# A hand-written issue order redone: fp32 products ahead of the first up-projection, and up-projections listed apart from their relu

## The chip, the cores and the metric

The program runs on one core of a Trainium2 chip. The metric is device time in microseconds (us), lower is better. A core has five engines that each work through their own list of instructions in order: TensorE (PE in the profile, its weight loads PEld), VectorE (DVE), ScalarE (ACT), GpSimd (POOL) and SyncE (SP, which here only starts transfers). Engines wait for each other through semaphores alone. PE writes its results to PSUM, eight banks of 512 fp32 columns; DVE and ACT read them from there.

## What is computed

A chunked state-space scan feeds a feed-forward layer with a squared relu.

```python
# scan: batch 4, 8 heads, 768 positions, 32 values per head, 16 state entries
L = np.exp(cum[:, :, :, None] - cum[:, :, None, :]) * causal
M = np.einsum('bhin,bhjn->bhij', Cc, Bc) * L
y = np.einsum('bhij,bhjd->bhid', M, xc) + np.einsum('bhin,bhnd->bhid', Cc, state) * decay_to_i
state = decay_full * state + sum_j(Bc * xc * decay_from_j)
# feed-forward: 3072 tokens, 256 -> 2048 -> 256
h = np.maximum(x @ w_in, 0.0)
out = (h * h) @ w_out
```

## The kernel before

The 3072 tokens are cut into 12 units of 256 positions: three stretches (j) of each of four sequences (b), in the order `UNITS` (line 86). Units 0 to 7 hold two positions per partition, units from `LATE` = 8 on one.

The decays come first. Rows `a` are loaded in two parts: `a_nat64` (what units 0 to 3 need) and `a_nat128` (the late rows, four transfers). `clamp` (line 591) clips them into `a_cl`, `scan` (line 520) multiplies them up along the positions into `cp`, and `prep_p` (line 484) turns `cp` into columns with small fp32 products on PE. ACT copies these to `P_sb` (and the totals to `Ptot`), DVE takes reciprocals into `Pinv`, POOL spreads `Ptot` into `Pquad`. For the late rows the fp32 products are lines 494, 499 and 607, the token `p2`.

A unit then goes through these steps. C times its decay (`prep_c`, line 167) and B (`prep_b`, lines 175 and 179) are laid into a tile `jt`; x times the inverse decay goes into `xs` (`prep_x`, line 187). `jt` is transposed into `bct`: units 0 to 3 by PE and copies out of PSUM (lines 205, 218, 220), later units by a transfer (line 196). PE multiplies B against C into four PSUM banks (lines 229, 235), and the result is masked into `mts`, a quarter at a time: by DVE straight from PSUM (line 244), or by an ACT copy `sc` (line 249) and a multiplication from there on DVE or POOL (line 253). One PSUM region of two banks then gathers, through line 260, the carry from the state (`Sd` against `bct`), the unit's own state update and `mts` against `xs`. ACT or DVE copies it out as `T`, the input of the feed-forward layer, and as `us`, the state update; DVE adds `us` into the running state `z` (lines 354, 359), and POOL spreads `z` into `Sd` (line 370; the first ones DVE, line 382). The next unit of the same sequence needs both `Sd` tiles of the unit before.

The feed-forward layer of unit n has eight up-projections of 512 hidden columns in PSUM (line 442, four matmuls each), a relu on ACT (line 447) into `hb`, of which the pool has four buffers (`fpool`), a square on DVE (line 453) into `h2` (eight buffers), and eight down-projections (line 469) that add up in one bank, copied out by ACT (line 476) and stored by SP.

All of this stands in the order of a long string, `ORDER` (line 48), read token by token by `one` (line 729) under a manual schedule: each token appends its instructions to the lists of its engines. So the string sets the order on every engine, and nothing else does. The tokens that matter here:

- `a0` to `l7`: up-projection and relu of unit 0 (a), 1 (b) and so on; `qa0`: its square; `A0`: its down-projection
- `fa`, `la`: loads of the early and late decay rows; `ac`, `sk`: clamp and scan; `sp`, `p2`: fp32 products of early and late rows; `pp`, `pd`: the pick ahead of `p2` and the two ACT copies behind it
- `ldC`, `ldB`, `ldx`, `ld`: loads of a unit; `gB3`: a POOL memset into the buffer of B of unit 3, which the load of that buffer, and every load behind it on SP, must wait for; `wi`, `wo`: loads of a quarter of the two weight matrices, started by POOL
- `jz`: a `jt` tile cleared; `ti`, `mb`: the triangle on POOL and its copy into `mask`; `pi`, `ku`, `ef`, `eb`: small masks made by POOL
- `pc`, `pb`, `px`: `prep_c`, `prep_b`, `prep_x`; `tr`, `tc`: transposes and their copies; `mt`: B against C; `mk`, `sc`, `ms`: a quarter masked directly, copied, masked from the copy
- `u`, `ina`, `inb`, `ca`: state update, `mts` against `xs` (two quarters each), carry; `t`, `us`: the copies out of the region; `rg5`: all of that for unit 4 with the B against C of unit 5, as one stretch of PE work
- `za`, `zb`, `sa`, `sb`: first and second `z` and `Sd` of a unit; `id15:128`: 15 matmuls on constants, 128 columns each, whose results nobody reads
- a letter behind a colon names the engine: v DVE, a ACT, p POOL, s SP

PSUM banks come from a list in turn (`bank`, line 398); a bank is skipped while the order holds it as busy. An instruction on a bank waits for the last reader of what was there.

Of the kernel before, what the change touches and what calls it, by code (L numbers as in the profile page):

```python
# [30 lines left out]
def kernel(  # L31
# [14 lines left out]
    NH, S, D, N = 8, 768, 32, 16  # L46
    NU = 12
    ORDER = """
        fa1:a jz0:v ef jz1:p id12:128 ti fa0:s la0:s id15:128 pi eb ldB0:s ac0:v ldC0:a sk0 ku sp la1:a pbh0:p hd
        id1:256 pc0:v pbl0:v mb:a id7:128 trC0 ps iv:8:16 tcC0:1:a tcC0:0:v trB0 la2:s tcB0:2:v pk id4:128 iv1:0:8  # L50
        id2:256 ldx0:s mt0 wi0 la3:s px0:v ldC1:s ac1:p su id8:128 ldB1:s wi1 ldx1:s u0:67 mk0 mk0 mk0 pc1:p sc0 pb1:a
        tr1 to id5:256 tc1:1:a tc1:0:v jz2:a ms0:p sk1 fq sf0 wo0 wi2 px1:p mt1 ina0 inb0 ca0 mk1 mk1 t0:aa sc1 us0
        pp1:a mk1 a0 ldC2:s a1 u1 ina1 ms1:v pc2 inb1 p2 pd sf1 ca1 t1:va us1 a3 qa1 ldB2:s qa0 wo1 wi3 a2 wo2 b0 qa3
        qb0 b1 qb1 fr b2 b3 A0 A1 B0 pb2:p B1 tr2 zb0 qb3 b4 a4 iv:32:64 zb1 tc2:1:v qa2 tc2:0:v b5 sb1 sb0 qb4 ldx2:s
        a5 qb2 qa4 mt2 gB3 sc2 ldB3:s ldC3:s B3 iv:16:32 px2 mk2 sc2 A3 ms2:v A2 mk2 qa5 a6 b6 ms2:p B2 a7 qb5 pb3:a
        qa6 b7 A5 u2 ina2 ldx3:s inb2 sf2 wo3 pc3 px3 ld4 A4 tr3 ca2 tc3:1:v t2:aa B4 us2 B5 tc3:0:v u3:45 pc4 mt3 us3
        sc3 c5 qb7 qb6 mk3 za3 pb4 ld5 c3 qa7 c4 qc5 c0 tr4 qc3 px4 pb5 sa3 c1 c6 ld6 qc4 pc5 tr5 qc0 A6 px5 pq A7 wm
# [6 lines left out]
        mk8 h0 qg7 G4 pc10 pb10 px10 ld11 h1 qh0 G5 mk8 h2 qh1 G6 h3 qh2 G7 rg9 za9 zb9 sa9 sb9 h4 qh3 H0 mk9 tr10 h5
        qh4 H1 mk9 h6 qh5 H2 h7 qh6 H3 mk9 i0 qh7 H4 pc11 pb11 px11 i1 qi0 H5 mk9 i2 qi1 H6 i3 qi2 H7 rg10 za10 zb10
        sa10 sb10 i4 qi3 I0 mk10 tr11 i5 qi4 I1 mk10 i6 qi5 I2 i7 qi6 I3 mk10 j0 qi7 I4 j1 qj0 I5 mk10 j2 qj1 I6 j3
        qj2 I7 rg11 za11 zb11 sa11 sb11 j4 qj3 J0 mk11 j5 qj4 J1 mk11 j6 qj5 J2 j7 qj6 J3 mk11 k0 qj7 J4 k1 qk0 J5
        mk11 k2 qk1 J6 k3 qk2 J7 rg12 k4 qk3 K0 k5 qk4 K1 k6 qk5 K2 k7 qk6 K3 l0 qk7 K4 l1 ql0 K5 l2 ql1 K6 l3 ql2 K7
# [366 lines left out]
    def mm1(blk, fp):  # L435

        h = bank()
        gi, o = group_of(WIN, fp)
        w = w_in_b[gi]
        for i in range(2):  # L440
            for g in range(2):
                nc.tensor.matmul(pp[:, h, i * 256:(i + 1) * 256],  # L442
                                 _fap(w, g * w.shape[2] + (o // 2) * 512 + 2 * (o % 2) + i, [[4, 128]]),
                                 T[blk][:, g].rearrange("p r u t -> p (r u t)"),
                                 start=(g == 0), stop=(g == 1), skip_group_check=True)
# [392 lines left out]
```

## Time and profile before

| | |
|---|---|
| three runs | 114.81, 115.22 and 118.83 us; median 115.22 |
| profiled execution | 115.38 us, of which the instructions span 113.7 us |
| PE busy | 107.4 us of the span |
| DVE, ACT, POOL busy | 83.9, 77.0 and 53.5 us |
| moved by transfers | 13.46 MB, mean 118 GB/s |
| first up-projection begins | 12.35 us into the span |

Instructions of the profile are named by engine, source line and tiles; "issue" is time for which the profile shows no wait. A line with several instructions gives their count behind an x and the time from the first one's start to the last one's end, or, in grouped views, their busy sum.

### The profile page before, as it was taken

The page shows a single profiled execution, that of the slowest core. Times are in us where ns is not written, and L with a number is a line of the kernel's source. Part 1 is how long each engine was busy: PE and PEld are TensorE (multiplying, and loading weights), DVE is VectorE, ACT ScalarE, POOL GpSimd, SP SyncE. Part 2 cuts the span into 40 slices and gives each one's busy share as a digit, 9 for nine tenths or more (in the row PEclk, how much of TensorE's full clock was granted, in tenths as well). Part 3 has the DMA queues.
Part 4 walks back from the last instruction along what each step waited for, and adds up shares of the span by engine and source line. Part 5 has one row for each costly group of instructions (what it writes and reads, how often), then busy time and mean ns, then how long its engine had stood idle before and what let it go on. Part 6 is the DMA issues. An engine that isn't in the chain of part 4 may idle for free.

```text
span 113.7 us, 3874 instructions
## 1 busy us (share of the span) xinstructions
PE 107.4 (95%) x1554; PEld 96.1 (85%) x1554; DVE 83.9 (74%) x185; ACT 77.0 (68%) x158; POOL 53.5 (47%) x99
## 2 busy tenths in 40 slices
PE   7976799999999999999999999999999999999980
PEld 7854699897998989989989989989899899899970
DVE  2597757997899799999856989669488398354440
ACT  1564875866894785685687687777876867867840
POOL 7689960599199926889401858057020020000000
PEclk9999999999999999999999999999999999999999
DMA  2999999399999909969799787960091030110202
GB/s 39 200 163 206 236 204 164 59 199 172 177 138 188 281 5 208 180 66 236 71 170 152 86 196 93 129 160 8 0 144 23 0 101 0 37 55 0 98 0 92
DMA packets 60690, 13.46 MB, mean 118 GB/s; under 512 B 56768, under 2 KB 59136, under 8 KB 60672
## 3 DMA queue, kind: packets, MB, share of 16 engines
q1 hardware_dynamic: 57728, 10.88, 53.4%
q0 software_dynamic: 1664, 2.10, 11.3%
q10 hardware_dynamic: 1280, 0.23, 1.1%
q8 instruction: 12, 0.20, 0.7%
q14 instruction: 6, 0.05, 0.1%
HBM read 10.58 MB, written 3.15 MB: 121 GB/s over the span
## 4 chain that ended last, share of the span: by engine, by line
PE 87%; POOL 3%; DMA 3%; SPq 2%; issue 1%; ACT 1%; DVE 0%; ACTq 0%
PE pp L442 38%; PE pp L469 37%; PE pp L260 7%; DMA a_nat<-in_a_dram 3%; PE pp L235 2%; PE pp L229 1%; POOL mts L253 1%; SPq L627 1%; SPq L134 1%; POOL jt L167 1%; PE pp L205 1%; POOL w_in_b L148 1%; ACT T L218 0%; DVE Sd L382 0%; POOL a_cl L592 0%
## 5 line engine op out<-in xcount | busy, mean ns | idle before, releaser
L447 ACT ACTIVATE hb<-pp 128x512 bf16<-128x512 f32 x96 | 54.6, 603 | 21.9 <-PE pp L442 19.4
L453 DVE TENSOR_TENSOR h<-hb 128x512 bf16<-128x512 bf16 x96 | 46.2, 500 | 12.7 <-ACT hb L447 12.4
L442 PE MATMUL pp<-T,w_in_b 128*128 128x256 bf16 x384 | 53.3, 273 | 0.7 <-ACT T L218 0.6
L469 PE MATMUL pp<-w_out_b,h 128*128 128x256 bf16 (+1 forms) x400 | 53.8, 268 | 0.0
L442 PEld LDWEIGHTS <-w_in_b 128*128 128x128 bf16 x384 | 41.4, 114 | 2.8 <-issue 1.9
L469 PEld LDWEIGHTS <-h 128*128 128x128 bf16 x400 | 37.7, 98 | 4.3 <-issue 0.6
L244 DVE TENSOR_TENSOR mts<-pp,mask 128x512 bf16<-128x512 f32 x43 | 28.5, 677 | 0.9 <-PE pp L235 0.9
L370 POOL TENSOR_TENSOR Sd<-z,Pquad 128x256 bf16<-128x256 f32 x16 | 10.7, 673 | 31.4 <-DVE z L354 22.4
L187 POOL TENSOR_TENSOR xs<-x_nat,Pinv 128x256 bf16<-128x256 f32 (+1 forms) x19 | 14.6, 786 | 3.9 <-DMA x_nat<-in_x_dram 2.7
L167 POOL TENSOR_TENSOR jt<-C_nat,P_sb 128x128 bf16<-128x128 f32 x22 | 9.6, 456 | 0.0
L528 PE MATMUL pp<-const-bfloat16-1.0 128*128 128x128 bf16 (+1 forms) x54 | 6.1, 286 | 0.8 <-PEq L822 0.8
L354 DVE SCALAR_TENSOR_TENSOR z<-z,Ptot,us 128x64 f32<-128x64 f32 x8 | 2.4, 294 | 6.1 <-ACT us L338 5.3
L476 ACT COPY osb<-pp 128x512 f32<-128x512 f32 x11 | 6.4, 583 | 0.4 <-PE pp L469 0.4
L260 PE MATMUL pp<-mts,xs 64*32 64x128 bf16 (+1 forms) x320 | 5.7, 219 | 0.5 <-DVE Sd L382 0.5
L528 PEld LDWEIGHTS <-const-bfloat16-1.0 128*128 128x128 bf16 x54 | 4.9, 128 | 1.0 <-issue 0.8
L175 POOL CAST jt<-B_nat 128x256 bf16<-128x256 f32 x9 | 4.4, 490 | 1.1 <-DMA B_nat<-in_B_dram 1.0
L260 PEld LDWEIGHTS <-xs 64*32 64x32 bf16 (+1 forms) x320 | 3.9, 91 | 0.9 <-issue 0.7
L260 PE MATMUL pp<-bct,Sd 128*128 128x128 bf16 x40 | 4.2, 219 | 0.0
L321 ACT CAST T<-pp 128x512 bf16<-128x512 f32 x4 | 2.3, 586 | 1.8 <-PE pp L260 1.5
L235 PE MATMUL pp<-bct 32*64 32x256 bf16 x128 | 3.4, 280 | 0.0
L260 PEld LDWEIGHTS <-Sd 128*128 128x128 bf16 x40 | 3.1, 100 | 0.3
L205 PE MATMUL pp<-eye_b,jt 128*128 128x128 bf16 x24 | 2.4, 220 | 1.1 <-POOL jt L167 0.5
...
## 6 DMA issues: line engine op xcount, KB each, us to landing
out_dram<-osb SPq DMA_DIRECT2D x11, 256.0 KB, 2.3
x_nat<-in_x_dram SPq DMA_DIRECT2D x8, 256.0 KB, 4.6
...
w_in_b<-in_moe_w_in_dram POOLq DMA_DIRECT2D x4, 256.0 KB, 5.8
w_out_b<-in_moe_w_out_dram POOLq DMA_DIRECT2D x4, 256.0 KB, 4.9
...
```

What stands on the lines that cost most here:

```text
L167: eng.tensor_tensor(out=_fap(jt[k % 3], 128 + 144 * g, [[384, 2], [32, 4], [1, 16]]), in0=_fap(loaded[k]["C"], 128 * g, [[16, 2], [32, 4], ...
L187: eng.tensor_tensor(out=_fap(xs, 256 * r, [[256, 2 // n], [32, 8], [1, 32]]), in0=_fap(loaded[k]["x"], 32 * r, [[32, 2 // n], [64, 8], [1, ...
L235: nc.tensor.matmul(pp[64 * u:64 * u + 64, q, r * 256:r * 256 + 256], bct[32 * q:32 * q + 32, r, 0, u * 64:u * 64 + 64], _fap(bct[32 * q:32 ...
L244: nc.vector.tensor_tensor(out=live[k]["mts"][:, q].rearrange("p r g i -> p (r g i)"), in0=pp[:, q, :], in1=mask1 if k >= LATE else mask, o ...
L260: nc.tensor.matmul(dst, w, v, start=bool(need), stop=False, skip_group_check=True, **({} if pos is None else {"tile_position": pos}))
L370: nc.gpsimd.tensor_tensor(out=_fap(S_d, 0, [[128, 2], [32, 4], [1, 32]]), in0=_fap(z, 0, [[32, 2], [0, 4], [1, 32]]), in1=_fap(Pquad, 4 * ...
L442: nc.tensor.matmul(pp[:, h, i * 256:(i + 1) * 256], _fap(w, g * w.shape[2] + (o // 2) * 512 + 2 * (o % 2) + i, [[4, 128]]), T[blk][:, g].r ...
L447: nc.scalar.activation(out=hb.rearrange("p i t -> p (i t)"), in_=pp[:, h, :], func=AF.Relu)
L453: nc.vector.tensor_tensor(out=h2, in0=hb, in1=hb, op=ALU.mult)
L469: nc.tensor.matmul(dst, h2[:, i, r * 128:(r + 1) * 128], w_out_b[gi][:, 2 * o + i, c0:c1], start=first, stop=(fp == 7 and i == 1), skip_gr ...
L476: nc.scalar.copy(out=osb, in_=pp[:, 6 if blk == 1 else 7, :])
L528: nc.tensor.matmul(pp[:, h, 0:int(cols)], ones_b[:, 0:128], ones_b[:, 0:int(cols)] if dep is None else dep, start=True, stop=True, skip_gr ...
```

## The change

The tokens up to the ninth unit's scan (to the `mk7` and `F3` near the middle of the string) are written in another order; from `F4` on the string is the same. Two tokens are new: `xa0` is the up-projection alone, `ra0` its relu alone, and the bank between them is held as busy. They are used for units 0 to 3.

```diff
@@ ORDER, first lines @@
-        fa1:a jz0:v ef jz1:p id12:128 ti fa0:s la0:s id15:128 pi eb ldB0:s ac0:v ldC0:a sk0 ku sp la1:a pbh0:p hd
-        id1:256 pc0:v pbl0:v mb:a id7:128 trC0 ps iv:8:16 tcC0:1:a tcC0:0:v trB0 la2:s tcB0:2:v pk id4:128 iv1:0:8
-        id2:256 ldx0:s mt0 wi0 la3:s px0:v ldC1:s ac1:p su id8:128 ldB1:s wi1 ldx1:s u0:67 mk0 mk0 mk0 pc1:p sc0 pb1:a
-        tr1 to id5:256 tc1:1:a tc1:0:v jz2:a ms0:p sk1 fq sf0 wo0 wi2 px1:p mt1 ina0 inb0 ca0 mk1 mk1 t0:aa sc1 us0
-        pp1:a mk1 a0 ldC2:s a1 u1 ina1 ms1:v pc2 inb1 p2 pd sf1 ca1 t1:va us1 a3 qa1 ldB2:s qa0 wo1 wi3 a2 wo2 b0 qa3
-        qb0 b1 qb1 fr b2 b3 A0 A1 B0 pb2:p B1 tr2 zb0 qb3 b4 a4 iv:32:64 zb1 tc2:1:v qa2 tc2:0:v b5 sb1 sb0 qb4 ldx2:s
-        a5 qb2 qa4 mt2 gB3 sc2 ldB3:s ldC3:s B3 iv:16:32 px2 mk2 sc2 A3 ms2:v A2 mk2 qa5 a6 b6 ms2:p B2 a7 qb5 pb3:a
+        eb fa0:s la2:s fa1:a la0:s ac0:v id15:128 id13:128 ldB0:s ldC0:a la3:s pi ldC1:s ldx0:a jz0:p ldB1:s sk0 jz1:p
+        ef sp hd id9:128 pc0:v trC0 iv1:0:8 la1:a pk ku ti mb:a pbh0:p pbl0:v trB0 ps iv:8:16 tcC0:0:v tcB0:2:v wi0
+        wi1 tcC0:1:a mt0 su px0:v id5:128 mk0 mk0 ac1:v mk0 pc1 id4:128 sc0 to u0:67 fq pb1:a tr1 tc1:0:v sf0 sk1
+        tc1:1:a ms0:p wo0 pp1:a ldx1:s px1 mt1 inb0 ina0 ca0 p2 wi2 t0:aa mk1 mk1 xa0 sc1 pd xa1 mk1 ms1:v u1 ra1 ina1
+        inb1 ra0 xa2 sf1 ca1 t1:vv ldC2:s jz2:p qa0 us1 ra2 wo1 qa1 us0 pc2 xa3 xb0 rb0 qb0 ra3 qa3 xb1 rb1 qb1 fr wi3
+        xb2 rb2 qa2 xb3 A0 A1 xb4 ldB2:s B0 xa4 zb0 pb2:v tr2 rb3 qb3 gB3 rb4 ra4 xb5 tc2:1:a tc2:0:v xa5 B3 B1 ldx2:s
+        iv:32:64 ra5 qb2 qb4 mt2 wo2 zb1 sb0 iv:16:32 rb5 ldB3:s qa4 ldC3:s sc2 mk2 A3 mk2 qa5 xa7 sb1 sc2 px2:v
+        ldx3:s xa6 ms2:p ra6 xb7 xb6 B2 ms2:v qb5 A5 A2 u2 qa6 ld4 ina2 inb2 wo3 rb7 sf2 rb6 qb6 pb3:p ra7 pc3 tr3 A4
...
@@ ORDER, units 2 to 7 (first the lines before, then after) @@
-        c2 B6 c7 C0 ms3:v mk3 qc6 mk3 qc7 afC2 pc6 pb6 B7 C3 C6 C4 qc1 bk rg4 C1 qc2 d1 d0 za4 sa4 mk4 mk4 d3 mk4 C5
-        d4 qd0 d2 mk4 px6 C2 C7 ld7 zb4 qd1 sb4 qd2 qd3 zb3 rg5 sb3 D0 tr6 mk5 za5 zb5 sa5 sb5 D1 iv:64:96 mk5 d5 qd4
-        D2 pb7 d6 qd5 d7 qd6 D3 zb2 e0 qd7 mk5 e1 qe0 sb2 D4 mk5 D5 ld8 pc7 e2 qe1 D6 e3 qe2 px7 ml D7 rg6 e4 qe3 za6
+        mk3 C0 afC2 pb6 qc6 C4 qc7 rc1 C3 qc1 B7 mk3 C6 qc2 bk rg4 za4 C1 xd1 sa4 rd1 xd0 rd0 px6 C5 mk4 xd3 rd3 xd4
+        mk4 qd0 rd4 xd2 mk4 rd2 qd3 C2 C7 zb3 mk4 rg5 qd2 qd1 pc6 zb4 d5 ld7 sb4 mk5 iv:64:96 za5 D0 e1 d6 mk5 sa5 mk5
+        pc7 tr6 e0 D1 d7 D2 zb5 sb5 qd4 qd6 qd5 qe1 mk5 pb7 ml qd7 ld8 zb2 D3 e2 qe0 e3 qe3 D6 D4 px7 sb2 D5 rg6 D7
...
@@ mm1 @@
+        return h
+
+    def relu(blk, fp, h):
         hb = fpool.tile([128, 2, 256], BF16, tag="hb", name=f"hb{blk}_{fp}")
         nc.scalar.activation(out=hb.rearrange("p i t -> p (i t)"), in_=pp[:, h, :], func=AF.Relu)
         hbs[(blk, fp)] = hb
@@ one @@
                 if name.islower():
-                    mm1(blk, k)
+                    relu(blk, k, mm1(blk, k))
...
+            if name[0] in "xr" and len(name) == 2 and name[1] in "abcd":
+                blk = "abcd".index(name[1])
+                if name[0] == "x":
+                    ups[blk, k] = mm1(blk, k)
+                    busy.add(ups[blk, k])
+                else:
+                    busy.discard(ups[blk, k])
+                    relu(blk, k, ups[blk, k])
+                return
```

Some steps change their engine too: the clamp of the late rows goes from POOL to DVE, `xs` of units 2 and 3 and the cast of B of unit 2 from POOL to DVE, half of `T` of unit 1 from ACT to DVE, half of `bct` of units 2 and 3 from DVE to ACT, the cast of B of unit 3 from ACT to POOL, the clearing of one `jt` from DVE to POOL and of another from ACT to POOL. The load of x of unit 0 goes from SP's queue to ACT's. There are 46 matmuls on constants instead of 54.

More of the change, by code (lines that the diff above doesn't have):

```diff
@@ L64 @@
[L64 to L68, printed above, removed]
@@ new lines @@
+        sa3 pb5 xc4 xc0 qb7 rc4 qc5 rc0 qc0 tr4 ld6 qc3 px4 pc5 xc2 rc2 A6 B6 qc4 A7 px5 wm tr5 xc6 xc1 rc6 xc7 rc7
+        mk3 C0 afC2 pb6 qc6 C4 qc7 rc1 C3 qc1 B7 mk3 C6 qc2 bk rg4 za4 C1 xd1 sa4 rd1 xd0 rd0 px6 C5 mk4 xd3 rd3 xd4
+        mk4 qd0 rd4 xd2 mk4 rd2 qd3 C2 C7 zb3 mk4 rg5 qd2 qd1 pc6 zb4 d5 ld7 sb4 mk5 iv:64:96 za5 D0 e1 d6 mk5 sa5 mk5
+        pc7 tr6 e0 D1 d7 D2 zb5 sb5 qd4 qd6 qd5 qe1 mk5 pb7 ml qd7 ld8 zb2 D3 e2 qe0 e3 qe3 D6 D4 px7 sb2 D5 rg6 D7
+        sb3 za6 px8 qe2 sa6 e4 e5 pc8 tr7 e7 qe4 e6 mk6 E0 mk6 f2 E3 mk6 f4 f0 zb6 E4 qe7 qe5 f1 qe6 f3 E6 qf1 E5 qf0
@@ new lines @@
+        E2 mk6 E1 ld9 E7 qf2 pb8 tr8 rg7 za7 mk7 f6 F0 f5 F2 F1 qf4 qf6 f7 g0 qf5 qf3 qf7 zb7 sa7 sb7 sb6 mk7 F3 mk7
+        F4 pc9 pb9 px9 ld10 g1 qg0 F5 mk7 g2 qg1 F6 g3 qg2 F7 rg8 za8 zb8 sa8 sb8 g4 qg3 G0 mk8 tr9 g5 qg4 G1 mk8 g6
+        qg5 G2 g7 qg6 G3 mk8 h0 qg7 G4 pc10 pb10 px10 ld11 h1 qh0 G5 mk8 h2 qh1 G6 h3 qh2 G7 rg9 za9 zb9 sa9 sb9 h4
+        qh3 H0 mk9 tr10 h5 qh4 H1 mk9 h6 qh5 H2 h7 qh6 H3 mk9 i0 qh7 H4 pc11 pb11 px11 i1 qi0 H5 mk9 i2 qi1 H6 i3 qi2
+        H7 rg10 za10 zb10 sa10 sb10 i4 qi3 I0 mk10 tr11 i5 qi4 I1 mk10 i6 qi5 I2 i7 qi6 I3 mk10 j0 qi7 I4 j1 qj0 I5
@@ L70 @@
+        mk10 j2 qj1 I6 j3 qj2 I7 rg11 za11 zb11 sa11 sb11 j4 qj3 J0 mk11 j5 qj4 J1 mk11 j6 qj5 J2 j7 qj6 J3 mk11 k0
+        qj7 J4 k1 qk0 J5 mk11 k2 qk1 J6 k3 qk2 J7 rg12 k4 qk3 K0 k5 qk4 K1 k6 qk5 K2 k7 qk6 K3 l0 qk7 K4 l1 ql0 K5 l2
+        ql1 K6 l3 ql2 K7 l4 ql3 L0 l5 ql4 L1 l6 ql5 L2 l7 ql6 L3 ql7"""
     LATE = 8
@@ L718, in late_banks @@
             busy.difference_update(turn)
-        squares = []
+        ups = {}
         def dep(name):
```

7 lines of the change are left out of this document (1 added, 6 removed).

## The prediction

> **What bounds the kernel now.** I read the page's engine sums first, then busy time by stretch, then PE's waits.
>
> ```profile
> PE 107.4 (95%) x1554; PEld 96.1 (85%) x1554; DVE 83.9 (74%) x185; ACT 77.0 (68%) x158; POOL 53.5 (47%) x99
> ```
>
> ```profile
> core 0: us, PE busy (x) PEld busy (x) DVE busy (x) ACT busy (x) POOL busy (x), PEclk, DMA share, GB/s
> 8.00:12.35 4.35, 2.52 (x61) 1.66 (x62) 3.56 (x8) 2.03 (x7) 4.32 (x8) 1.00 1.26 205
> 12.35:50.00 37.65, 37.57 (x654) 33.48 (x654) 32.95 (x72) 27.75 (x61) 26.33 (x46) 1.00 0.92 163
> 50.00:108.00 58.00, 58.00 (x714) 52.88 (x712) 41.75 (x91) 42.18 (x82) 16.80 (x29) 1.00 0.50 88
> ```
>
> ```profile
> PE pp L442 <- ACT T L218: 0.6, 1, 0.6
> ```
>
> The columns of the second view are stretch, length, busy time of each engine (with its instructions), clock and transfers. The last row is all that PE waits for after 12.4 us. So the profile has two parts. Up to 12.35 us, where the first up-projection starts, PE is fed through a chain over all engines. After it PE is busy 37.57 of 37.65 us and then 58.00 of 58.00: it never waits. From this follows the frame of the forecast. An order can gain only by starting the first up-projection earlier or by moving PE work ahead of it; everything behind can only get worse. The span is 113.7 us, and the profiled execution took 115.38 us, 1.68 more; that is 0.16 above the median of the three runs. I forecast against 115.38.
>
> **The start.** These are the rows of DVE, ACT and POOL from the timeline ahead of 12.35 us (start, length, instruction), with the ends of two DVE waits.
>
> ```profile
> 0.90 0.29 POOL L532 TENSOR_SCALAR_AFFINE_SELECT eye_f<-const-float32-1.0 128x128 f32<-128x128 f32 x1 [0.40 <-POOLq L822]
> 1.14 0.73 POOL L569 MEMSET jt<- 128x768 bf16 x1
> 1.83 1.19 POOL L532 TENSOR_SCALAR_AFFINE_SELECT tri<-const-bfloat16-1.0 64x128 bf16<-64x128 bf16 x4
> 2.64 0.22 DVE L592 TENSOR_SCALAR a_cl<-a_nat 64x128 f32<-64x128 f32 x1 [1.32 <-DMA a_nat<-in_a_dram]
> 3.38 0.20 POOL L532 TENSOR_SCALAR_AFFINE_SELECT pick<-pick 128x16 f32<-128x16 f32 x1
> ...
> 3.65 0.62 ACT L562 COPY mask<-tri 128x512 bf16<-128x512 bf16 x1
> 5.07 0.21 ACT L762 COPY P_sb<-pp 128x64 f32<-128x64 f32 x1 [0.80 <-DVE jt L167]
> 5.31 0.25 DVE L620 RECIPROCAL Pinv<-P_sb 128x16 f32<-128x16 f32 x1 [0.20 <-ACT P_sb L762]
> 5.61 0.51 DVE L220 COPY bct<-pp 128x256 bf16<-128x256 bf16 x2
> 6.33 0.69 DVE L187 TENSOR_TENSOR xs<-x_nat,Pinv 128x512 bf16<-128x512 f32 x1
> 6.94 1.88 DVE L244 TENSOR_TENSOR mts<-pp,mask 128x512 bf16<-128x512 f32 x3
> 9.54 0.36 DVE L220 COPY bct<-pp 128x384 bf16<-128x384 bf16 x1 [0.73 <-PE pp L205]
> 9.82 0.73 DVE L521 TENSOR_TENSOR_SCAN cp<-a_cl,const-float32-0.0 128x128 f32<-128x128 f32 x1
> 10.61 0.42 DVE L382 TENSOR_TENSOR Sd<-pp,Pquad 128x256 bf16<-128x256 f32 x1
> ...
> 11.65 0.65 ACT L218 CAST T<-pp 128x256 bf16<-128x256 f32 x2 [0.80 <-PE pp L260]
> 12.82 0.34 ACT L596 ACTIVATE pick_p<-pick,cp 128x16 f32<-128x16 f32 x1
> ```
>
> In the new order POOL makes the triangle last: ahead of it stand two clears of `jt` (2 x 0.73) and six small selects (0.20 to 0.29 each, 1.2 to 1.7 together). From 0.90 us that puts the triangle's end (1.19) at 4.75 to 5.3 us; I take 4.95. ACT is listed mask, then `P_sb`: 4.95 + 0.62 + 0.21 = 5.8 us, and only then can DVE take the reciprocal that it took at 5.31. So this piece loses half a microsecond. From there DVE decides: reciprocal 0.25, two copies 0.51, `xs` 0.69, three masks 1.88, the clamp that comes over from POOL (0.22, the smaller clamp's row), the copy of `bct` 0.36, `Sd` 0.42, scan 0.73, together 5.06, ending at 10.9 us. The two DVE waits of before in this stretch (0.73 at the copy, and for `Pquad`, which is now listed ahead of POOL's masking) are filled. Then ACT makes the pick (0.34) and both halves of `T` (0.65): the first up-projection starts at 11.9 us instead of 12.35, a gain of 0.45. The bounds are 11.3 (starts overlap by 0.05 to 0.1 us in these rows) and 12.4 (each of some eight crossings between engines costs up to 0.06 more).
>
> The chain of waits shows `p2` on the path behind the first two up-projections:
>
> ```profile
> 12.35 1.03 PE pp L442 x8
> 13.39 0.57 PE pp L260 x45
> 13.96 0.36 PE pp L494 x8
> 14.32 0.23 PE pp L499 x8
> 14.56 0.33 PE pp L607 x2
> ```
>
> 0.36 + 0.23 + 0.33 = 0.92 us. In the new order it runs while ACT makes pick and `T` (0.99 us), so all 0.92 leave the path; if that cover were short, the rest would come back. Together the start gives 1.37 us.
>
> Edits at nothing: the clears of `jt` and the cast of B of unit 3 that come to POOL (0.73 and less) lie where POOL is busy 26.33 of 37.65 us; fewer matmuls on constants. The load of x of unit 0 goes to ACT's queue, and behind it one late row waits there until an early row has landed; that costs nothing, because the late rows' clamp stands behind two masks, and were it late, DVE's chain would shift by as much. SP's loads of units 1 and 2 start sooner without it, and the second quarter of `w_in` starts sooner without the clamp ahead of it on POOL; both move up alike, so I leave the early weights where they were.
>
> **What the weights get.** `gB3` holds back every load behind B of unit 3. These rows are POOL's last `w_in` start and the memset, SP's wait for it, and the transfer queues in two stretches (packets, MB, share of 16 engines; q0 carries the weights, q1 SP's loads), with the landing time of the last `w_in`.
>
> ```profile
> 14.42 0.71 POOL L148 DMA_DIRECT2D w_in_b<-in_moe_w_in_dram  x1
> ...
> 21.14 0.09 POOL L143 MEMSET B_nat<- 128x1 f32 x1
> ```
>
> ```profile
> SPq L134 <- POOL B_nat L143: 10.6, 1, 10.6
> ```
>
> ```profile
> q0 software_dynamic: 575, 0.63, 62.6%
> q1 hardware_dynamic: 3677, 0.66, 62.2%
> ```
>
> ```profile
> q0 software_dynamic: 842, 1.08, 106.8%
> ...
> w_in_b<-in_moe_w_in_dram POOLq DMA_DIRECT2D x1, 256.0 KB, 6.5
> ```
>
> The first queue pair is 8 to 14 us, the second row 14 to 20. In the old order the memset stands behind two `Sd` that wait for DVE, so it comes at 21.14, and from 14 us on the weights have the engines to themselves: 0.18 MB per us. Beside SP's loads they had 0.105. In the new order the memset stands right behind the start of the last `w_in`, at some 15 us, and nothing holds it; SP's loads of units 3 to 5 run from about 16. The last `w_in` landed at 14.42 + 6.5 = 20.9 us. From 16 to 20.9 the weights moved 0.89 MB, of which up to 0.25 was the quarter of `w_out` started after it. At 0.105 the same 0.64 to 0.89 MB take 6.1 to 8.4 us: it lands at 22.1 to 24.4.
>
> When does PE ask for it?
>
> ```profile
> 23.26 0.87 PE pp L442 x8
> ```
>
> That row is `a6` and `b6`, the first users. In the new order the same products stand ahead of the first user `xa7`, less `p2` and less one down-projection (0.44, half this row): 23.26 - 0.45 - 0.92 - 0.44 = 21.45 us. So PE, which never waited here, waits 0.65 to 2.95 us; nothing excludes zero either if SP's loads come in gaps. I take 1.2, nearer the low end, because the quarter was started before the next one and SP's issues leave gaps. On the page "DMA: Bandwidth & Descriptors" of the Trainium skill, section "Queues, rings and completion order", each transfer engine goes round the queues packet by packet. Read with the profile's packets (1.1 KB for the weights, 0.18 for SP) the weights would keep some six sevenths of the bytes and this term would be about zero; the rows show equal bytes and equal time, and I go by them.
>
> **DVE.** It takes over two `xs` (2 x 0.69), a cast of B, half of a `T`, and gives two `bct` copies (2 x 0.36) to ACT.
>
> ```profile
> 14.32 0.41 DVE L220 CAST T<-pp 128x256 bf16<-128x256 f32 x1
> 15.68 0.43 POOL L175 CAST jt<-B_nat 128x256 bf16<-128x256 f32 x1
> ```
>
> 1.38 + 0.43 + 0.41 - 0.72 = 1.5 us more, where it had 37.65 - 32.95 = 4.7 us free, most of it early. Its squares are also listed in clumps: up to six relus stand ahead of their squares with four `hb` buffers (never more than four before), so a relu, `e0` say, waits for the square of `d4`, behind two masks. Between zero (the free time covers it) and 1.5 (all on the path) I take 0.6, the place where the next `mk` or square ends last.
>
> **Sum.** -0.45 - 0.92 + 1.2 + 0.6 = +0.43: 115.8 us. Its own range, with a wait for weights of 0.5 to 2 us, is 115.1 to 116.6.
>
> **Rivals.** First, nothing is given back: SP's loads leave the weights their rate and DVE's free time covers its work. Then 1.37 us stay: 114.0. For it speaks that PE waited for nothing in the old order; against it that its cover was the late gate.
>
> Second, the ungated loads decide: the wait at `xa7` takes its upper 2.95 and DVE its 1.5, -1.37 + 4.45 = +3.1: 118.5. It makes the kernel slower by over 2% once that quarter of `w_in` lands later than 24.5 us, or than 23.6 with DVE at its bound.
>
> Third, a cold array. At the start 27 products on constants take 0.11 us each, at 6.86 us eight take 0.08:
>
> ```profile
> 0.83 3.04 PE L528 MATMUL pp<-const-bfloat16-1.0 128*128 128x128 bf16 x27 [0.83 <-PEq L822]
> 6.86 0.64 PE L528 MATMUL pp<-const-bfloat16-1.0 128*128 128x128 bf16 x8
> ```
>
> If eight fewer let PE fall back to such a pace, 4 us of it would cost some 2 us: 117.8. Against it: from 8 to 12.35 us PE was busy just 2.52 of 4.35 us, and its first eight matmuls then took 1.03 us where a later eight take 0.87. The new order has about as much work there, so 3%. By the Trainium skill, page "TensorE: Matmul & The Clock Gate", Part 1, the clock falls back after an idle window of about 3.4 us; I see no such gap in the new order.
>
> Fourth, the start gains more than 2.3 us. That would need the first up-projection by 11.0 us with no later wait, where DVE's rows alone end at 10.9 and ACT's 0.99 follow: 5%, 112.9 or less.
>
> **Chances.** Forecast 0.48, nothing given back 0.22, loads decide 0.22, cold 0.03, large gain 0.05. The range of 8 in 10 runs from just under the first rival, 113.9, to 118.2, which takes in most of the second. About 2% is what a measurement of this kernel can tell from no change: under 112.9 us faster, over 117.5 slower. Slower holds most of the second rival, the third, and a tail of the forecast: 0.25. Faster is the fourth and a bit of the first: 0.06. Within 2%: 0.69.
>
> **What would show it.** Right: `p2` on PE ahead of the first L442; that L442 at 11.3 to 12.4 us; the memset on `B_nat` near 15 us with q1 and q0 both busy from 16 on; a PE wait ahead of an L442 near 21.5 to 24 us that ends with a transfer of `w_in`; short PE waits for DVE masks or squares between 25 and 60 us. Wrong: no PE wait near 22 us (first rival), or a wait there much longer than 2 us; PE rows of L442 well over their steady pace just after the start (third); or PE waiting elsewhere, for `bct` transfers or state products, which I cost at nothing.

## The result and the profile after

The changed kernel takes 121.78 us (median of four runs, 120.6 to 122.37), the kernel before 115.33 us (114.81 to 118.83, four runs): 1.056 times as long, with a 95% interval of 1.045 to 1.067. The profiled execution took 122.37 us, with a span of 120.6. The array's clock falls in some executions of the kernel before too, which then take 117 to 120 us, and the comparisons leave those out.

The page's sum of busy time and its row of PE's granted clock in 40 slices:

```profile
PE 110.5 (92%) x1546; PEld 97.1 (80%) x1546; DVE 87.1 (72%) x187; ACT 77.1 (64%) x155; POOL 52.3 (43%) x98
...
PEclk9965555999999999999999999999999999999998
```

Busy time by stretch shows where the array's work took longer and where it stood idle (length, busy time of each engine with its instructions, granted clock, transfers):

```profile
4.00:12.00 8.00, 4.72 (x72) 3.30 (x70) 5.82 (x11) 3.32 (x10) 5.98 (x13) 0.69 1.04 176
12.00:20.00 8.00, 6.54 (x130) 4.48 (x131) 5.08 (x11) 2.88 (x8) 4.46 (x9) 0.50 1.12 187
20.00:62.00 42.00, 40.63 (x622) 35.99 (x621) 38.26 (x79) 30.39 (x63) 25.28 (x43) 0.99 0.75 138
```

Three things are new. From 4 to 12 us PE does 4.72 us of work. From 12 to 20 us its clock is at half. From 20 to 62 us it idles 42.00 - 40.63 = 1.37 us; in the kernel before that was 0.07:

```profile
20.00:62.00 42.00, 41.93 (x696) 37.38 (x695) 37.41 (x78) 30.41 (x65) 27.48 (x47) 1.00 0.90 155
```

PE's waits, by who ended them (total, times, longest):

```profile
PE pp L236 <- DVE bct L221: 3.0, 2, 2.7
PE pp L206 <- POOL jt L180: 1.7, 1, 1.7
...
PE pp L206 <- ACT hb L451: 0.6, 1, 0.6
PE pp L443 <- ACT hb L451: 0.4, 1, 0.4
PE pp L261 <- DVE mts L245: 0.3, 1, 0.3
```

The first row leads to DVE, whose timeline (start, length, instruction) is this at the place of the wait:

```profile
6.43 0.23 DVE L180 CAST jt<-B_nat 128x128 bf16<-128x128 f32 x1 [1.46 <-DMA B_nat<-in_B_dram]
...
9.46 3.08 DVE L596 TENSOR_SCALAR a_cl<-a_nat 128x128 f32<-128x128 f32 x1
12.46 0.68 DVE L245 TENSOR_TENSOR mts<-pp,mask 128x512 bf16<-128x512 f32 x1
13.06 0.34 DVE L221 COPY bct<-pp 128x384 bf16<-128x384 bf16 x1
```

The clamp of the late rows is on record with 3.08 us. POOL in the same time:

```profile
9.46 0.23 POOL L592 TENSOR_TENSOR Pquad<-Ptot,quad 128x32 f32<-128x32 f32 x1
9.66 1.14 POOL L254 TENSOR_TENSOR mts<-sc,mask 128x512 bf16<-128x512 bf16 x1
10.76 0.61 POOL L153 DMA_DIRECT2D w_out_b<-in_moe_w_out_dram  x1
11.38 1.06 POOL L188 TENSOR_TENSOR xs<-x_nat,Pinv 128x512 bf16<-128x512 f32 x1
12.38 0.76 POOL L149 DMA_DIRECT2D w_in_b<-in_moe_w_in_dram  x1
```

POOL works there without a gap, and the clamp ends at 12.54, just behind POOL's `xs` (12.44). The copy of `bct` starts at 13.06 instead of 9.54, and the first up-projection at 16.41 instead of 12.35:

```profile
14.96 0.64 PE L498 MATMUL pp<-eye_f,cp 128*64 128x32 f32 x8
15.41 0.62 PE L503 MATMUL pp<-eye_f,cp 128*64 128x32 f32 x8
15.96 0.61 PE L611 MATMUL pp<-pick_p,spread 128*128 128x16 f32 x2
16.41 1.87 PE L443 MATMUL pp<-T,w_in_b 128*128 128x256 bf16 x8
```

The late products stand ahead of it, as forecast, but they and the eight matmuls behind them go at half pace (1.87 us, before 1.03). The span is 6.9 us longer: 16.41 - 12.35 = 4.06 of it ahead of the first up-projection, 2.85 behind it, although 0.92 us of products moved ahead.

The clock changes at 7.08 and 20.74 us:

```profile
3.67:7.08 3.41, 1.72 (x27) 1.24 (x24) 1.30 (x7) 2.21 (x6) 1.43 (x7) 1.00 1.09 196
7.08:20.74 13.66, 10.61 (x185) 7.30 (x184) 10.14 (x17) 4.31 (x12) 9.33 (x16) 0.50 1.09 180
```

The stretch of 3.41 us in which PE was busy for 1.72 holds the gap of 1.7 us from PE's second wait. Half clock then lasted 13.66 us, four times 3.41.

### The profile page after: what moved, and what is told of

The parts are those of the page before. It is cut to its first block, busy times and chain, and to the rows that moved or that the text cites. A ratio compares the mean times of both kernels' runs of the same rounds, so it can differ in the third digit from the quotient of the medians.

```text
span 120.6 us, 3849 instructions
## 1 busy us (share of the span) xinstructions
PE 110.5 (92%) x1546; PEld 97.1 (80%) x1546; DVE 87.1 (72%) x187; ACT 77.1 (64%) x155; POOL 52.3 (43%) x98
## 4 chain that ended last, share of the span: by engine, by line
PE 67%; DVE 18%; DMA 4%; issue 3%; ACT 3%; SPq 2%; ACTq 0%
PE pp L443 28%; PE pp L473 28%; DVE h L457 7%; DVE mts L245 7%; PE pp L261 6%; DMA C_nat<-in_C_dram 4%; SPq L135 2%; PE pp L236 2%; ACT hb L451 2%; PE pp L230 1%; DVE z L360 1%; DVE a_cl L596 1%; DVE z L355 1%; PE pp L206 1%; DVE xs L188 1%
## 5 line engine op out<-in xcount | busy, mean ns | idle before, releaser
L443 PE MATMUL pp<-T,w_in_b 128*128 128x256 bf16 x384 | 55.1, 279 | 0.5 <-ACT hb L451 0.4
L457 DVE TENSOR_TENSOR h<-hb 128x512 bf16<-128x512 bf16 x96 | 46.0, 498 | 11.5 <-ACT hb L451 11.0
L443 PEld LDWEIGHTS <-w_in_b 128*128 128x128 bf16 x384 | 41.9, 115 | 3.6 <-issue 2.2
L371 POOL TENSOR_TENSOR Sd<-z,Pquad 128x256 bf16<-128x256 f32 x16 | 11.3, 711 | 39.9 <-DVE z L355 25.1
L188 POOL TENSOR_TENSOR xs<-x_nat,Pinv 128x256 bf16<-128x256 f32 (+1 forms) x17 | 12.5, 752 | 1.6 <-DMA x_nat<-in_x_dram 1.6
L168 POOL TENSOR_TENSOR jt<-C_nat,P_sb 128x128 bf16<-128x128 f32 x22 | 10.3, 491 | 0.4 <-DMA C_nat<-in_C_dram 0.4
L261 PE MATMUL pp<-mts,xs 64*32 64x128 bf16 (+1 forms) x320 | 6.3, 236 | 0.3 <-DVE mts L245 0.3
L532 PE MATMUL pp<-const-bfloat16-1.0 128*128 128x128 bf16 x46 | 4.9, 292 | 0.8 <-PEq L835 0.8
L596 DVE TENSOR_SCALAR a_cl<-a_nat 64x128 f32<-64x128 f32 (+1 forms) x2 | 3.4, 1680 | 2.8 <-DMA a_nat<-in_a_dram 2.8
L532 PEld LDWEIGHTS <-const-bfloat16-1.0 128*128 128x128 bf16 x46 | 4.3, 138 | 0.9 <-issue 0.8
L236 PEld LDWEIGHTS <-bct 32*64 32x64 bf16 x128 | 1.3, 110 | 4.1 <-DVE bct L221 3.5
L250 ACT CAST sc<-pp 128x512 bf16<-128x512 f32 x5 | 2.8, 591 | 2.7 <-PE pp L236 2.6
```

The source lines that it names most:

```text
L168: eng.tensor_tensor(out=_fap(jt[k % 3], 128 + 144 * g, [[384, 2], [32, 4], [1, 16]]), in0=_fap(loaded[k]["C"], 128 * g, [[16, 2], [32, 4], ...
L188: eng.tensor_tensor(out=_fap(xs, 256 * r, [[256, 2 // n], [32, 8], [1, 32]]), in0=_fap(loaded[k]["x"], 32 * r, [[32, 2 // n], [64, 8], [1, ...
L236: nc.tensor.matmul(pp[64 * u:64 * u + 64, q, r * 256:r * 256 + 256], bct[32 * q:32 * q + 32, r, 0, u * 64:u * 64 + 64], _fap(bct[32 * q:32 ...
L261: nc.tensor.matmul(dst, w, v, start=bool(need), stop=False, skip_group_check=True, **({} if pos is None else {"tile_position": pos}))
L371: nc.gpsimd.tensor_tensor(out=_fap(S_d, 0, [[128, 2], [32, 4], [1, 32]]), in0=_fap(z, 0, [[32, 2], [0, 4], [1, 32]]), in1=_fap(Pquad, 4 * ...
L443: nc.tensor.matmul(pp[:, h, i * 256:(i + 1) * 256], _fap(w, g * w.shape[2] + (o // 2) * 512 + 2 * (o % 2) + i, [[4, 128]]), T[blk][:, g].r ...
```

## The experiments

Eighteen kernels were run. Medians are over all executions of a kernel, ratios are to the kernel before on the same chip, with their 95% interval. Line numbers shift by a few from kernel to kernel: L441 to L443 are up-projections, L452 to L457 squares.

**The clamp, earlier on DVE.**

```diff
-mk0 mk0 ac1:v mk0
+mk0 mk0 mk0
-pbh0:p pbl0:v
+pbh0:p ac1:v pbl0:v
```

> The changed kernel, with the late rows' clamp still on DVE but listed ahead of the cast of B of unit 0, where DVE waits 1.46 us for B and POOL has nothing to do; nothing else moves. Theory A (the clamp took 3.08 us because POOL worked beside it without a gap, and DVE's chain moved by that): the clamp takes 0.2 to 0.4 us, the first up-projection starts near 13.6 us instead of 16.41, and the time is 118.5 to 120 us, less than the whole 2.8 us if the array is still at half clock up to 20 us. Theory B (a fp32 clamp of this size is that slow on DVE, or waits for its rows): it takes some 3 us here too, and the time stays at 121 to 122. Theory C (the half clock alone sets the time): the start moves up, the clock is still 0.5 from 8 to 20 us, and the time stays over 121.

```profile
6.64 0.23 DVE L596 TENSOR_SCALAR a_cl<-a_nat 128x128 f32<-128x128 f32 x1 [1.38 <-DMA a_nat<-in_a_dram]
...
11.36 1.31 DVE L525 TENSOR_TENSOR_SCAN cp<-a_cl,const-float32-0.0 128x128 f32<-128x128 f32 x1
```

120.3 us, ratio 1.041 [1.034, 1.048]. The same instruction takes 0.23 us where POOL does no more than end a cast (at 6.76 us), so theory B falls. The scan behind it took 1.31 us, where it takes 0.41 elsewhere, beside a POOL `xs` that ran from 11.32 to 12.38. PE's gap for B stayed, the clock was at half from 7.96 to 18.20 us, and the first up-projection came at 14.49 us. The expectation of theory A missed on two counts: the start came later than 13.6, and the time lies just above its range.

**The load of B of unit 0 ahead of the late rows.** (On SP the changed kernel has it behind two of them, the kernel before behind one.)

```diff
-fa0:s la2:s fa1:a la0:s
+fa0:s fa1:a ldB0:s la2:s la0:s
-id13:128 ldB0:s ldC0:a
+id13:128 ldC0:a
```

> The changed kernel, with the load of B of unit 0 issued on SP second, as before the change, ahead of two late rows. The clamp stays where it is. Expected if the late landing of B is what opens PE's gap of 1.7 us: DVE's cast of B starts near 5.0 instead of 6.43 us, the gap is gone, the first w_in starts near 5.8 instead of 7.08. If the gap is what lets the clock fall (theory C), the clock stays 1.00 and the time falls by 2 to 4 us, to 118 to 120. If the clamp alone decides (theory A), the clamp still takes 2 to 3 us, and the time falls by 1.1 at most, to 120.7 or more.

```profile
5.23 0.16 DVE L180 CAST jt<-B_nat 128x128 bf16<-128x128 f32 x1
...
8.39 1.06 DVE L596 TENSOR_SCALAR a_cl<-a_nat 128x128 f32<-128x128 f32 x1
...
10.57 1.27 DVE L525 TENSOR_TENSOR_SCAN cp<-a_cl,const-float32-0.0 128x128 f32<-128x128 f32 x1
```

118.47 us, ratio 1.024 [1.016, 1.033]. The cast moves from 6.43 to 5.23 and the first up-projection to 13.35 us, three microseconds earlier, two of them because the clamp now met POOL's `mts` alone (8.21 to 9.36) and took 1.06. The clock fell all the same: the stretch from 3.71 to 7.13 us had PE busy for 2.43 of 3.42 and no longer the gap of 1.7. So the time lies in the range that theory C gave, but not for its reason.

**The clamp on DVE in the kernel before.**

```diff
-la3:s px0:v ldC1:s ac1:p su
+la3:s px0:v ldC1:s su
-mk0 mk0 mk0 pc1:p
+mk0 mk0 mk0 ac1:v pc1:p
```

> The kernel before, with one token moved: the late rows' clamp on DVE behind the third mask instead of on POOL, where POOL then works without a gap. Theory A: the clamp takes 1.5 to 3.5 us there too, the first up-projection starts at 14 to 15 us instead of 12.35, and the time is 117 to 118.5 us. Theory B (slow on DVE by itself): about 3 us too. If the 3.08 us come from something else in the changed kernel (rows that land late): 0.2 to 0.4 us, and 115 to 115.6 us.

```profile
8.54 0.45 DVE L592 TENSOR_SCALAR a_cl<-a_nat 128x128 f32<-128x128 f32 x1
...
13.29 0.26 PE L260 MATMUL pp<-xs,jt 64*32 64x64 bf16 x16 [1.03 <-POOL xs L187]
```

115.57 us, ratio 1.000 [0.995, 1.005]. Here the clamp took 0.45 us and not theory A's 1.5 to 3.5: it ended at 8.99, just behind a POOL `mts` (7.76 to 8.90). Whether it comes through behind one POOL instruction or four differs from place to place. The first up-projection began at 11.23 us, 1.1 earlier, and all of it went into a PE wait of 1.03 us for `xs` of unit 1.

**The gaps filled, nothing else.**

```diff
-pc0:v trC0 iv1:0:8
+pc0:v trC0 id18:128 iv1:0:8
-px1 mt1 inb0
+px1 id24:128 mt1 inb0
```

> The changed kernel with 42 more matmuls on constants of 128 columns: 18 ahead of the transposes of B of unit 0 and 24 ahead of B against C of unit 1, where PE had gaps of 1.7 and 2.7 us. No other engine's list changes. Theory C (the half clock sets the time): the clock stays near 1.00, PE's work from 13 to 20 us takes half, and the time falls to 117.5 to 119.5. Theory A (the clamp sets it): the clock may stay at 1.00, but the first up-projection still starts at 15.3 or later and the time falls by 1 to 1.5 at most, the rest going into later waits of PE.

```profile
4.46:7.87 3.41, 2.84 (x52) 2.19 (x51) 2.00 (x8) 1.43 (x6) 1.62 (x5) 1.00 1.11 202
...
13.96 1.03 PE L443 MATMUL pp<-T,w_in_b 128*128 128x256 bf16 x8
...
16.18 0.63 PE L443 MATMUL pp<-T,w_in_b 128*128 128x256 bf16 x4 [0.61 <-DMA w_in_b<-in_moe_w_in_dram]
```

Ratio 1.025 [1.016, 1.034]. Its executions at full clock took 118.42 and 118.27 us, one whose clock fell 121.17. A fourth took 184.18 us at a mean clock of 0.569; it has no trace, and what happened in it is open. So constants do not keep the clock in every execution. That one of 121.17 prices the fallen clock at some 2.8 us within one kernel, and at full clock constants alone take back 3.4 of the 6.4 us; part of that is the clamp, which took 2.16 us here instead of 3.08. The second row shows a start at 13.96 us, the third a wait of 0.61 for an early quarter of `w_in`, whose load started late behind B of unit 0.

**All three mended at once** (base of the runs below; its clamp is on POOL between the first two `w_in`).

```diff
-fa0:s la2:s fa1:a la0:s
+fa0:s fa1:a ldB0:s la2:s la0:s
-id13:128 ldB0:s ldC0:a
+id13:128 ldC0:a
-wi0 wi1 tcC0:1:a mt0
+wi0 ac1:p wi1 tcC0:1:a id12:128 mt0
-mk0 mk0 ac1:v mk0
+mk0 mk0 mk0
-pb1:a tr1
+pb1:a id8:128 tr1
-px1 mt1 inb0
+px1 id12:128 mt1 inb0
```

> The changed kernel with its start mended in three places at once: the load of B of unit 0 second on SP; the late rows' clamp on POOL between the first two w_in, as before the change; 32 more matmuls on constants in PE's three gaps. Everything from the first up-projection on stays as in the changed kernel. If late B, the blocked clamp and the half clock are the whole loss of the start, the clock stays 1.00 from about 5 us on, the first up-projection starts at 11.8 to 12.6 us with the late products ahead of it, and what is left of the loss is the later waits of some 1.3 us less the late products moved: 115.4 to 116.6 us, within 1% of the kernel before. Rival (the start was the only loss, the later waits only come with it): 114.3 to 115. Rival (something else in the new order costs): over 117.

```profile
12.96 1.03 PE L442 MATMUL pp<-T,w_in_b 128*128 128x256 bf16 x8
...
20.00:62.00 42.00, 40.51 (x680) 35.39 (x678) 36.31 (x75) 29.47 (x60) 25.25 (x44) 1.00 0.92 150
```

117.4 us, ratio 1.017 [1.011, 1.023]: above the expected 116.6, in the range of the rival that something else in the new order costs. The start is whole: with the late products done the first up-projection begins at 12.96 us, which is 0.3 less than the 12.35 + 0.92 of the kernel before, and all six executions kept about the full clock. What is left lies behind it. From the first up-projection to the end of the span there are 116.1 - 12.96 = 103.1 us, in the kernel before 113.7 - 12.35 - 0.92 = 100.4. Of these 2.7 us some 1.5 are PE's idle time, 1.49 us from 20 to 62 us as in the changed kernel. The other 1.2 are time in which PE counts as busy, 98.3 us instead of 97.1 for the same products; no run explains them. The next runs look for the cause of the idle time.

**Eight relu buffers.**

```diff
-fpool = ctx.enter_context(tc.tile_pool(name="fpool", bufs=4))
+fpool = ctx.enter_context(tc.tile_pool(name="fpool", bufs=8))
```

> The kernel of the run above with eight buffers for the relu's output instead of four, nothing else. If the clumped squares make relus wait for buffers and PE wait for the relus (PE's 0.6 at the transposes near 28 us, ended by a relu, and part of the rest), those waits go and the time is 0.4 to 1.0 us under the run above. Rival (DVE's own throughput sets it, the buffers only show it): the relu comes sooner, but PE waits as long for squares or masks behind, and the time is the same within 0.3.

```profile
PE pp L472 <- DVE h L456: 0.7, 1, 0.7
...
PE pp L442 <- DMA w_in_b<-in_moe_w_in_dram: 0.4, 1, 0.4
PE pp L260 <- DVE xs L187: 0.4, 1, 0.4
```

117.94 us, ratio 1.022 [1.018, 1.026]. PE's wait for the relu is gone, and it waits for DVE's square and `xs` instead. The buffers only showed it.

**The early gate in the kernel before.**

```diff
-wo1 wi3 a2
+wo1 wi3 gB3 a2
-mt2 gB3 sc2
+mt2 sc2
```

> The kernel before, with the POOL memset on B of unit 3 moved up to right behind the start of the last w_in, as in the changed kernel; PE's list is the same. It measures the price of the early gate alone, where PE asks for the last w_in at 23.26 us. By the forecast's term: the memset comes near 15 us, SP's loads share the transfers with w_in, the last w_in lands at 22 to 24.4, PE waits 0 to 1.2 us and the time is 115.4 to 116.6. Rival (SP's loads leave the weights their rate, or come too slowly to matter): no PE wait near 23 us and 115.0 to 115.5.

116.02 us, ratio 1.005 [1.001, 1.009]. The last `w_in` landed 6.5 us after its start, as before, and PE did not wait for it. PE's one new wait behind the start, 0.4 us for a mask of DVE, came at 30.68 us.

**The late products ahead, in the kernel before.**

```diff
-mk1 mk1 t0:aa
+mk1 mk1 pp1:a p2 t0:aa
-us0 pp1:a mk1 a0
+us0 mk1 a0
-inb1 p2 pd
+inb1 pd
```

> The kernel before, with only the pick and the fp32 products of the late rows moved ahead of the first up-projection. By the forecast's term they lie beside ACT's pick and both halves of T: 0.9 us leave the path, and the time is 114.3 to 114.7. Rival (they fill only the 0.6 us that PE waited for T there, or hold the first up-projection back): 114.8 to 115.6.

118.54 us, ratio 1.026 [1.020, 1.032]: both expectations missed, and the one edit that the forecast put at a gain of 0.92 us costs some 3. The trace is of an execution whose clock had fallen (121.55 us); the five at full clock, by which the ratio goes, have none. In it PE waited 0.7 us for an `sc` copy and 0.6 and 0.5 for relus that it did not wait for before. The products take their PSUM bank earlier, and the banks behind are dealt otherwise; that this is the reason is argued, not shown.

**The kernel before with more constants.**

```diff
-pb1:a tr1
+pb1:a id6:128 tr1
-px1:p mt1 ina0
+px1:p mt1 id8:128 ina0
-mk1 a0
+mk1 id8:128 a0
```

> The kernel before with 22 more matmuls on constants, 128 columns each, in three places where PE waited ahead of the first up-projection (6, 8 and 8 of them); no other engine's list changes. If it is PE's thin work at the start that lets the clock fall, then this kernel keeps it: its executions stay together at 115.2 to 115.8 us, with none of those of 117 to 120 us that the kernel before shows when its clock falls. If the clock has nothing to do with PE's work there, such executions come as often as with the kernel before. If the added products hold the chain up, all its times go up by 0.3 to 0.8 us.

115.26 us; all twelve executions lie between 115.15 and 115.81 with a mean clock of 0.996 or more. Of the 19 of the kernel before beside them five took 119.1 to 119.3 us at a mean clock of 0.952 to 0.956. The ratio of the executions at full clock is 1.003 [1.001, 1.005]. This version beats the changed kernel, and the kernel before wherever that one's clock falls.

**What is lost behind the start.** Five more runs on the mended start, each with one suspect put back:

```diff
# xs of units 2 and 3 on POOL
-sc2 px2:v
+sc2 px2:p
-B5 px3:v tc3:0:v
+B5 px3:p tc3:0:v
# the gate late
-qb3 gB3 rb4
+qb3 rb4
-rb5 ldB3:s
+rb5 gB3 ldB3:s
# the kernel before's order behind fr
-fr wi3 xb2 ...
+fr wi3 ldB2:s wo2 b2 b3 A0 A1 ...
# each relu right behind its products
-xa0 sc1 pd xa1 ... ra1 ina1 inb1 ra0
+xa0 ra0 sc1 pd xa1 ra1 ... ina1 inb1
# all of DVE's new work back: px2:p px3:p as above and
-t1:vv
+t1:va
-pb2:v
+pb2:p
```

> The changed kernel with the mended start, and xs of units 2 and 3 on POOL again instead of DVE. It gives back the larger part of the work that DVE was handed (two pieces of 0.7 to 0.9 us). If DVE's load is what makes PE wait between 24 and 62 us, the waits there shrink by 0.6 to 1.6 us and the time comes to 115.8 to 116.8 us, from 117.4. Rival (the order of squares, masks and relus sets the waits, whatever the load; or POOL is now late with xs): 117 to 118.

> The changed kernel with the mended start, and the POOL memset on B of unit 3 moved back to just ahead of the load that it holds, behind the first sb, so that SP's loads of units 3 to 5 start some 6 us later and the weights have the transfers alone. By the price of the early gate in the kernel before (0.5%): 116.6 to 117.0 us. Rival (in the new order the later loads reach their users too late): 117.5 to 118.5. If the gate does not matter here: 117.2 to 117.6.

> The mended start of the changed kernel up to the token fr, with the late products ahead of the first up-projection, and from there on the kernel before's order word for word (with three tokens between, that its first part had already done: the last w_in, B of unit 2, the third w_out). If all that is still lost after the mended start comes from the order behind it, this kernel is at 115.0 to 115.8 us, even with the kernel before. If the start itself leaves a loss (late loads, a debt of DVE or ACT): 116.2 to 117.

> The changed kernel with the mended start, and each relu listed right behind its up-projection again (the 32 of units 0 to 3 that the change lists apart); all else in the changed order. If the relus listed late are what makes PE wait for banks and buffers after 24 us, about 1 us of the 2 comes back: 116.0 to 116.8 us, from 117.4. Rival (the squares and masks on DVE set the waits): 117.0 to 118.

> The changed kernel with the mended start, and all work that DVE was handed behind it put back: xs of units 2 and 3 and B of unit 2 on POOL, half of T of unit 1 on ACT. With the two xs alone the median was 116.97. If DVE's load is the rest of the loss: 115.8 to 116.6 us. Rival (the order, not the load): 116.8 to 117.5.

`xs` on POOL: 116.97 us, ratio 1.018 [1.014, 1.022]. Late gate: 117.42, 1.020 [1.017, 1.023]. Old order behind `fr`: 116.98, 1.017 [1.015, 1.020]. Relus joined: 118.67, 1.032 [1.029, 1.035]. All of DVE's work back: 117.04, 1.017 [1.015, 1.020]. Beside 1.017 for the mended start none of them takes the loss away. Listing the relus apart even helps: joined, the kernel is 1.5% slower. In the run with the old order a new PE wait of 0.9 us for a relu stood in B against C of unit 2, so the seam was measured along with that order. The late products ahead of the first up-projection, which alone cost 2.6% in the order before, stand in every one of these kernels: a run of the mended start with the products back in their old place is missing, and they remain a suspect.

**The same work handed to DVE in the kernel before.**

```diff
-iv:16:32 px2 mk2
+iv:16:32 px2:v mk2
-pc3 px3 ld4
+pc3 px3:v ld4
-pb2:p
+pb2:v
-t1:va
+t1:vv
```

> The kernel before, its order untouched, with the same work handed to DVE: xs of units 2 and 3 and B of unit 2 from POOL, half of T of unit 1 from ACT (1.4 to 2.2 us of DVE work in all). By the forecast's term, with DVE's load deciding: 0.5 to 1.5 us slower, 115.8 to 116.8. Rival (DVE's free time in this order covers it, so that the loss of the changed kernel needs its order too): 115.0 to 115.6.

```profile
25.26 0.60 PE L442 MATMUL pp<-T,w_in_b 128*128 128x256 bf16 x4 [1.98 <-DVE mts L244]
```

116.21 us, ratio 1.009 [1.006, 1.012]. In that order the work on DVE does cost 1 us: `xs` of unit 2 waits on DVE for its load, the masks stand behind it, and PE waits 1.98 us for a mask (an execution whose clock fell behind that gap).

**An earlier start in the kernel before.**

```diff
# both: x of unit 0 on ACT's queue, and constants as above (18 in the first kernel, 22 in the second)
-ldC0:a sk0
+ldC0:a ldx0:a sk0
-id2:256 ldx0:s mt0
+id2:256 mt0
# the first alone: the clamp on DVE
-ldC1:s ac1:p su
+ldC1:s su
-mk0 mk0 mk0 pc1:p
+mk0 mk0 mk0 ac1:v pc1:p
```

> The kernel before with three things that the runs so far point to: 18 more matmuls on constants ahead of the first up-projection; the late rows' clamp on DVE behind the third mask (in the run of that alone the first up-projection began at 11.23 us instead of 12.35, and PE then waited 1.03 us for xs of unit 1, whose x landed late); and the load of x of unit 0 on ACT's queue, so that SP starts the load of x of unit 1 about a microsecond sooner. If that load was what ate the earlier start, 0.7 to 1.1 us stay: 114.2 to 114.7 us. Rival (the start is eaten by the next thing that is late, POOL's or DVE's work on units 1 and 2): 115.0 to 115.6.

> The kernel before with 22 more matmuls on constants and the load of x of unit 0 on ACT's queue; the clamp stays on POOL. The control of the run above: if the load alone does it, 114.6 to 115.0; if it needs the clamp moved, 115.1 to 115.5 as with the constants alone.

115.94 us, ratio 1.006 [1.002, 1.010], and 115.9, ratio 1.005 [1.001, 1.008]. With the clamp on DVE the scan took 1.05 us, and the first up-projection came at 12.10 instead of 11.23. The load alone brings nothing. One of the first kernel's twelve executions took 118.67 us at a mean clock of 0.985, in spite of its 18 constants.

**POOL out of the way of two squares**, on the mended start.

```diff
-qb6 pb3:p ra7
+qb6 pb3:a ra7
-tc3:1:a pc4 ca2
+tc3:1:a ca2
-us3 mt3 sc3
+us3 mt3 pc4 sc3
```

> The changed kernel with the mended start, and POOL kept out of the way of two squares near 26 us: the cast of B of unit 3 on ACT again (so that POOL makes C of unit 3 some 0.8 us sooner), and C of unit 4 listed behind unit 3's B against C. In the run of the mended start POOL's four C products ran from 25.84 to 27.67 us, two squares on DVE took 1.92 us beside them where two take 0.8, a relu waited 1.10 for a square, and PE 0.6 for that relu. If POOL beside the squares is the cause, the two squares take 0.8 to 1.2 us, PE's wait of 0.6 at the transposes of unit 3 shrinks to 0 to 0.3, and the time is 0.3 to 0.6 us under the mended start's 1.017 of the kernel before: 1.011 to 1.014. Rival (the list of squares on DVE is simply too long there): the wait stays at 0.5 to 0.7 and the ratio at 1.015 to 1.02.

```profile
26.15 1.16 DVE L456 TENSOR_TENSOR h<-hb 128x512 bf16<-128x512 bf16 x2
...
27.51 0.49 PE L205 MATMUL pp<-eye_b,jt 128*128 128x128 bf16 x6 [0.61 <-ACT hb L450]
```

117.0 us, ratio 1.016 [1.011, 1.020]. C of unit 4 did not move on POOL, where nothing stood between; the cast on ACT alone shortened the two squares from 1.92 to 1.16 us. PE's wait stayed at 0.61, as the rival had it. But POOL did not get out of the way: its C products ran from 25.16 to 27.57 us. The relu that PE waits for starts just behind the first of the two squares, which took 0.62 us in both kernels and began at 26.08 and 26.15; only the second became shorter (0.62 instead of 1.38). So the length of the pair does not set the wait, and whether POOL beside the first square does is not tested.

## Why the prediction was wrong

**The frame held.** PE had no wait behind 12.4 us to lose, and behind the start the span only grew. By the terms of the sum: the start was forecast at -0.45 us and came out at +4.06; all behind it at -0.92 + 1.2 + 0.6 = +0.88 and came out at +2.85. The start is the step that failed, through the price of the clamp, the load of B and the clock; the terms behind it were too small by 2 us, with the half clock up to 20.74 us in that.

**The clamp.** "The clamp that comes over from POOL (0.22, the smaller clamp's row)" took 3.08 us. The row was from a place where POOL's selects did not hold it up; the new place was among POOL's densest work. The measured lengths (0.23 with POOL nearly at rest; 0.45, 0.47, 1.06, 2.16 and 3.08 beside it) show that the neighbour sets it. By the Trainium skill, page "SBUF — State Buffer", section "Who interferes with whom", VectorE and GpSimd share a port pair under an exclusive lock: a copy, cast or `tensor_scalar` in a two-port mode, or an instruction with two inputs from SBUF, waits until the other engine's instruction is done. The traces agree: where the clamp is long, and where the scan with its two inputs is (0.41 to 2.23 us), it mostly ends 0.1 to 0.3 us behind one of POOL's instructions. How many of them can pass in between the section does not say: the clamp of 3.08 us stood through four.

**The load of B of unit 0.** "I leave the early weights where they were" looked at what SP's list gains and passed over what it loses there: B moved behind a second late row, from 1.72 to 2.19 us at the issue. The cast then began at 6.43 instead of 4.89, the first `w_in` at 7.08 instead of 5.25. The run that moves B ahead of both is 3.3 us faster, together with what it changes for the clamp.

**The cold array** was a rival at 3%, with the wrong condition. Its size, some 2 us, is more than its rows give (4 us at 0.08 us a product become 5.5 at 0.11) and less than what was measured: 2.8 us in the changed kernel with more constants, some 4 in the kernel before (119.1 to 119.3 beside 115). "I see no such gap in the new order" rested on a start without late B. By the Trainium skill, page "TensorE: Matmul & The Clock Gate", Part 1, the clock is set by a free-running window of 3.41 us. The trace agrees in the lengths: 3.41 us at full, 13.66 at half. The page lets the clock fall after an idle window; the traces do not agree, for here it fell behind stretches with PE busy for 1.72 of 3.41 us and for 2.43 of 3.42, and in the kernel before with the clamp on DVE it stayed through one with 1.80:

```profile
10.55:13.96 3.41, 1.80 (x62) 1.53 (x60) 1.60 (x4) 2.46 (x7) 1.04 (x1) 1.00 1.24 198
```

A thin stretch is enough, and busy time alone does not tell which. One of the changed kernel's four runs shows a mean clock of 0.996 and took as long (122.13). But the record of the clock begins with a first change (at 3.67 us in the profiled execution, and the 28 constants ahead of it took 0.11 us each, the nine right behind it 0.08), and what lies ahead counts as full; so whether that run stood at half pace for longer stays open.

**The late products.** They run beside the pick and `T`, as forecast, but not wholly. In the mended start `T` ends at 12.73 us and the first up-projection starts at 12.96: 0.23 of the 0.92 stay on the path; at half clock it was 0.94. That the move costs something further behind was not in the forecast at all: alone, in the kernel before, it costs some 3 us.

**The weights.** The gate came at 15.86 us, near the forecast's 15; the wait of 1.2 us for the last `w_in` did not come. In the mended start, where PE is not late, this quarter landed at 21.3 us (14.94 + 6.4), and PE asked for it at 23.04; the forecast had 22.1 to 24.4 and 21.45. From 16 to 22 us of the changed kernel the two queues moved:

```profile
q0 software_dynamic: 816, 1.04, 100.0%
q1 hardware_dynamic: 1210, 0.16, 19.3%
```

The weights kept 1.04 of 1.20 MB, 87%. The packet-by-packet rule of the Trainium skill (page "DMA: Bandwidth & Descriptors", section "Queues, rings and completion order") gave six sevenths, and I set it aside for rows from another stretch. The trace agrees with the bytes here, though its packets are 816 to 1210 and not one for one, and with neither from 8 to 14 us of the kernel before (575 to 3677). SP's one load of x took 3.63 us to issue.

**DVE's term** of 0.6 had the right sign and was too small: PE idles 1.37 us from 20 to 62 us, and the mended start leaves a ratio of 1.017. Its two named parts are not the cause in the new order: undoing DVE's work or the four buffers does not take the loss away, nor does undoing the gate or the relus. PE waits there in pieces of 0.2 to 0.6 us for relus and masks, at other places in each version. What in the order makes them late is open; the late products ahead are the one suspect with a measured price (2.6% in the kernel before) that no run took back.

**An earlier start** was counted at its full length. Where it came about (11.23 us) the next late piece, `xs` of unit 1, took all of it.
